# A planner's tables made to change along the stream: 40 places, 332 entries

## The chip, the cores and the metric

The kernel runs on one core of one Trainium2 chip. The metric is the device time of one execution in microseconds (us), as the median of several. The core has a matrix engine (TensorE, PE in the profile; PEld is its weight load), VectorE (DVE), ScalarE (ACT), GpSimd (POOL) and SyncE (SP), which only issues DMAs here. Matmuls write to PSUM, which has eight banks of 512 fp32 columns; everything else lies in SBUF.

## What is computed

Two layers; each is an attention block and then a mixer block, both with a residual, on x of 2048 rows and 448 columns (16 heads of 28):

```
x = x + A(layernorm(x), wqkv, wo)          # qkv, softmax(q k^T / sqrt(28)) v, wo
x = x + B(layernorm(x), w1, w2, w3, w4)    # twice, with the same weights
...
B(x): h  = gelu(layernorm(x) @ w1)
      hs = (the 4 column quarters of h, shifted by -1, +1, -2, +2 rows) @ w2
      x1 = x + hs
      x1 + gelu(layernorm(x1) @ w3) @ w4
```

The gelu is the one with tanh. Each layer has 16 x 2048 x 2048 exponentials in its softmax.

## The kernel before, in words

**Work and tiles.** The 2048 rows are 16 tiles of 128. A layer's queries are cut into five chunks of 4, 4, 4, 2 and 2 tiles (CHUNKS), its keys into chunks of two to four tiles (KC), its heads into four groups of four (g). ORDER lists the segments: for a chunk and a range of key tiles, one segment for each head group. A block is one key step of one head, 512 score columns wide; the segments laid end to end give the stream of 2048 blocks.

**Score units.** `t_scores` (L1631) walks through the stream and takes two or three blocks at a time as a unit: units of even number have three PSUM banks, those of odd number two. The scores are matmuls of 32 rows each (`score_ops`, L1510), and `t_exp` (L1733) gives a unit to ACT as one exp of 1536 or 1024 columns (L1748). Unit u waits for the exp of unit u - 2. `t_pv` (L1770) multiplies the exps by the values (L1765) in the order of the stream; the exp of unit u waits for the product of unit u - 6.

**Exps on VectorE.** Some blocks are taken out of the stream ahead of time (`ahead_of`, L1642) and get their exp as a polynomial on VectorE: one eviction (`d_first`, L1590, instruction L1592) and a chain of four more (L1619, L1621, L1623, L1626). Such a block either takes the third bank of an even unit (rates in R_RATE) or an extra bank (rates in D_RATE).

**The rest of the work** goes on between the units. `t_q` (L1386) loads four normed tiles transposed by a DMA (`load_xT`, L1230, instruction L1233) and starts `q_proj` (L1290) for each head group: projection on PE (L915 with wq_pad), eviction (L1307), square on GpSimd (L1248), a statistic on PE, and an add on VectorE (L1336), after which the block's scores can run. Keys go the same way with a maximum at the end (kmaxc, L1275); from the maxima `t_bias4` (L1430) makes a bias, and where a segment continues a chunk with further keys, `t_qp` (L1527) updates the query block by it (L1532). The mixer tiles are transposed one by one (`tr_dma`, L1123, instruction L1125). `t_mixB` (L2109) multiplies by w3, collects the results of up to four tiles in a buffer, h2T or a second one that lies in free slots of vaug and kT (h2W), and applies one gelu to it (L2202), for which ACT loads another table and then the exp table again. Some gelus are made from a tanh on ACT and VectorE steps instead (TANHW; L2019 to L2022), which needs no table.

**What sets the order.** Nothing is written in program order by hand. Every step is a Python generator that yields operations with a guessed duration. `Sched.run` (L466) keeps a planned time for each engine and at each step places the operation that can start first, by its priority where several can. RANK gives priorities by step and chunk, read when a step is started; R_RATE, D_RATE, RLO, RHI, DLO, DHI, DTH, DDTH and DWIN decide which blocks go to VectorE; PE_NORM chooses a way to normalise; Sched.DOUBT and DOUBT2 add a margin when an engine waits for another or for a DMA (`ready_at`, L452); Sched.EARLY lets a buffer be taken ahead of its data. `keep_pe_busy` (L405) puts filler matmuls (L2248, on the identity matrix) into planned gaps of PE, as TARGET and WIN ask. The result is one fixed list of instructions for each engine, with semaphores; the durations are then whatever the chip takes. Tables and knobs are constants for the whole plan. MOVES and WEAVE, which could edit the finished queues, are empty.

Of the kernel before, what the change touches and what calls it, by code (L numbers as in the profile page):

```python
# [264 lines left out]
class Sched:  # L265
    LAT = {"pe": 0.23, "act": 0.175, "dve": 0.145, "pool": 0.2, "sp": 0.2}
    OWN = {"pe": 0.0, "act": 0.15, "dve": 0.125, "pool": 0.05, "sp": 0.05}
    DOUBT = {"dma": 0.6, "pool": 0.4, "dve": 0.15, "act": 0.1}
    DOUBT2 = {"dma": 0.0, "pool": 0.0, "dve": 0.0, "act": 0.0, "pe": 0.0}
    EARLY = 0.25  # L270
    AGED = 1.0
    WIN = 2.3
    TARGET = 0.6
    LWIN = 2.8
    LOW = 0.0
    LCRED = 0.3
# [343 lines left out]
DPRIO = 3.393  # L620
DST = [('dve', 0.6), ('dve', 0.6), ('dve', 0.34), ('dve', 0.6)]
DSEG = 1
R_RATE = {2: 0.098, 3: 0.111, 5: 0.018, 6: 0.032, 13: 0.059, 20: 0.074, 22: 0.151, 25: 0.029, 29: 0.117, 31: 0.032, 32: 0.075, 35: 0.032, 37: 0.17, 38: 0.078, 39: 0.176, 41: 0.012, 42: 0.198, 43: 0.169, 44: 0.03, 45: 0.075, 46: 0.091, 54: 0.061, 56: 0.176, 59: 0.044, 62: 0.186, 33: 0.131, 63: 0.12, 16: 0.143, 23: 0.089, 18: 0.193, 27: 0.155, 61: 0.058, 49: 0.137, 30: 0.2, 53: 0.018, 0: 0.165, 40: 0.083, 8: 0.165, 1: 0.086, 26: 0.092, 48: 0.062, 60: 0.16, 55: 0.021, 52: 0.098, 4: 0.093, 9: 0.052, 15: 0.099, 10: 0.063, 28: 0.082, 7: 0.162, 47: 0.2, 12: 0.141}
RLO = 5
RHI = 7
RPRIO = 1
DWIN = 1.714
DTH = 0.403
XSHUT = (10, 76)
DLO = 6  # L630
DHI = 12
DPK = 2
DDTH = 1.502
UPRIO = 1.991
# [13 lines left out]
DURG = 1  # L648
FASTKV = 3
SMALL = [11, 12]  # L650
W_POS = (12, 6, 16, 6, 5, 10, 33, 26)
# [17 lines left out]
FMD = 0.83  # L669
FMO = 1.59  # L670
SWT = 0.103
Sched.DOUBT = {'dma': 0.8, 'pool': 0.6, 'dve': 0.05, 'act': 0.05}
Sched.LCRED = 0.3


# [4 lines left out]
def build_kernel(nc, A_x, A_wqkv, A_wo, B_x, B_w1, B_w2, B_w3, B_w4, out, n_layers=2):  # L680
# [85 lines left out]
    with st:  # L766
# [864 lines left out]
        def t_scores():  # L1631
            yield from seg_ready(0, segs[0][4])
            for b in BANKS[0:3]:
                yield ("acq", [b])
            yield ("reserve", "act", True)
            yield ("sig", ("start",))
            cur = -1
            pos = 0
            u = 0
            taken = {}  # L1640

            def ahead_of(si0, kb0, rates, lo, hi, used):  # L1642
                for ahead in range(lo, hi):
                    si, kb = si0, kb0 + ahead
                    while si < len(segs) and kb >= len(seg_kb[si]):
                        kb -= len(seg_kb[si])
                        si += 1
                    if si > si0 + DSEG or si >= len(segs):
                        return None
                    L, ch, g = segs[si][0:3]  # L1650
                    rate = rates.get(seg_b0[si] // 32, 0)
                    if not rate:
                        return None
                    js = [j for j in range(4) if (si, kb, j) not in home and j not in used]
                    if taken.get((si, kb), 0) >= DPK or not js:
                        continue
                    if taken.get((si, id(rates), 0), 0) >= rate * (kb + 1) * 4:
                        continue
                    if any(("k", L, g, kc_of(L, kt)) not in SC.events for kt in seg_kb[si][kb]):
                        return None  # L1660
                    if si > si0 and (("q", L, CHUNKS[L][ch][0] // 4, g) not in SC.events or (not segs[si][5] and ("qp", si) not in SC.events)):
                        return None
                    return (si, kb, js[0])
                return None

            def take(blk, rates, slot):
                home[blk] = pbuf(slot)
                taken[(blk[0], id(rates), 0)] = taken.get((blk[0], id(rates), 0), 0) + 1
                taken[blk[0:2]] = taken.get(blk[0:2], 0) + 1

            ringed = set()
            while True:
                if u == 1:
                    yield ("acq", ["b3"])
                    yield ("acq", ["b4"])
                if u >= 2:
                    yield ("wait", ("ex", u - 2))
                if u - 2 in ringed:
                    yield ("wait", ("dx", u - 2))
                un = []  # L1680
                rb = None
                lim = 3 - u % 2
                while pos < len(stream) and len(un) < lim:
                    if len(un) == 2 and rb is None and SC.load("dve", DWIN) < DTH:
                        rb = ahead_of(un[-1][0], un[-1][1], R_RATE, RLO, RHI, [b_[2] for b_ in un])
                        got = None
                        if rb is not None:
                            got = yield ("try", [xtra("y") + YS, xtra("pd") + PDS])
                        if got is not None:
                            take(rb, R_RATE, got[1])  # L1690
                            ringed.add(u)
                            break
                        rb = 0
                    blk = stream[pos]
                    pos += 1
                    if blk in home:
                        continue
                    home[blk] = ("pt", 5 * ((u // 2) % 3) + 3 * (u % 2) + len(un))
                    un.append(blk)
                    si = blk[0]  # L1700
                    if si != cur:
                        cur = si
                        yield ("sig", ("segstart", si))
                    yield from seg_ready(si, seg_kb[si][blk[1]])
                if not un:
                    break
                units.append(un)
                blks, banks = list(un), [b_ for b_ in unit_banks(u)]
                extra = []
                si0, kb0, _ = un[-1]  # L1710
                at[0], at[1] = si0, kb0
                if u in ringed:
                    blks.append(rb)
                    banks.append(2)
                    extra.append((rb, ("b2", got[0], got[1], u)))
                if SC.idle_share(8.0) >= FTH and SC.load("dve", DWIN) < DDTH:
                    blk = ahead_of(si0, kb0, D_RATE, DLO, DHI, [b_[2] for b_ in blks])
                    if blk is not None:
                        got = yield ("try", [MISC[0:2], xtra("y") + YS, xtra("pd") + PDS])
                        if got is not None:  # L1720
                            take(blk, D_RATE, got[2])
                            blks.append(blk)
                            banks.append(bi(got[0]))
                            extra.append((blk, got))
                yield from score_ops(blks, banks)
                for blk, got in extra:
                    yield ("spawn", d_first(blk, *got), 1 if len(got) == 3 else RPRIO)
                yield ("sig", ("st", u))
                u += 1
            units.append([])  # L1730
            yield ("sig", ("st", u))
# [377 lines left out]
        def t_mixB(L, ch, tiles, direct, pr):  # L2109
# [12 lines left out]
            if direct:  # L2122
                yield from tr_pe(slots, xt)
                for xs in slots:
                    yield ("rel", xs)
            wide = False
            hname = None
            small = L == 0 and tiles == SMALL
            if small:
                yield ("wait", ("kvfree",))  # L2130
                hb = vaug[:, 9:16, :].rearrange("p a b -> p (a b)").rearrange("p (f w) -> p f w", w=NW)
                hkey = [[("vaug", 9 + k) for k in range(f * NW // 512, (f * NW + NW - 1) // 512 + 1)] for f in range(14)]
            elif direct:
                hb, hkey = PT, [[("pt", f)] for f in range(14)]
            else:
                hname = yield ("acq", ["h2T", "h2W"] if ("xdone", 1) in SC.events else ["h2T"], [("xT", xt)])
                wide = hname == "h2W"
                if wide:
                    hkey = [[("vaug", 9 + f)] if f < 7 else [("kT", g, 2 + f) for g in range(4)] for f in range(14)]
                else:  # L2140
                    hb, hkey = h2T, [[("h2T", f), ("xst",)] for f in range(14)]
# [4 lines left out]
                return vaug[:, 9 + f, 128 * i:128 * i + 128] if f < 7 else kT[:, i, 128 * (2 + f):128 * (3 + f)]  # L2146

            late = []
            soft = TANHW.get((L, tiles[0]), 0) and not direct
            fps = 512 // NW  # L2150
            parts = [list(range(f, min(f + fps, 14))) for f in range(0, 14, fps)]
            if wide:
# [89 lines left out]
        def t_final():  # L2242
            for t in range(NT):
                yield ("wait", ("x2", 1, t))
            yield op("sp", 0.05, lambda e: e.nop(), deps=odmas)
# [44 lines left out]
        SC.spawn(t_extra(0, 16), 3)  # L2290
        SC.spawn(t_extra(1, 9), 3)
        SC.spawn(t_final(), 9)
        est = SC.run()

        def again(fn, k):
            return lambda e: [x for _ in range(k) for x in fn(e)]
# [63 lines left out]
```

## Time and profile before

| | |
|---|---|
| median of 3 runs | 1028.55 us (1028.09 to 1029.22) |
| profiled execution | 1028.86 us |
| its span, first to last instruction | 1027.1 us |
| mean granted TensorE clock | 1.000 |
| PE, DVE, ACT, POOL busy | 973.3, 823.3, 980.3, 293.1 us |
| instructions | 38497 |

The profile is that of one execution. A row of its groups reads: line, engine, operation, what is written from what, shapes and count; then busy us in sum and mean ns of one; then idle time of the engine just before these instructions, and who released it. A row of the timeline reads: start, duration, instruction, count, and in brackets the idle time before it with its releaser. A row of the stretches reads: from and to, length, busy us of PE, PEld, DVE, ACT and POOL with counts, the granted clock, the DMA share and GB/s. Matmuls overlap, so PE's busy time is more than its work.

The order in which a build puts the instructions of each engine can be read from the build without a run. It is used below for both kernels.

### The profile page before, as it was taken

Reading aid. Unit: us, or ns where it says so; the run is one execution under the profiler, and the core shown is the slowest. Engines: PE = TensorE matmul, PEld = TensorE weight load, DVE = VectorE, ACT = ScalarE, POOL = GpSimd, SP = SyncE. Lnnn points to the kernel's source line nnn. Section 1 sums busy time; section 2 is a strip of 40 time slices with the busy share of each in tenths; the row PEclk is TensorE's granted clock in tenths of the full one; section 3 lists DMA queues with packets and bytes.
Section 4 is the critical chain, followed back from the end, with each engine's and each line's share of the span. In section 5 each row is a group of like instructions: output and inputs, shape, how many; then the busy total and the mean of one; then the engine's idle time right before and its main releaser. Section 6 shows DMA issues by size and latency. Waiting matters only on the chain.

```text
span 1027.1 us, 38497 instructions
## 1 busy us (share of the span) xinstructions
PE 973.3 (95%) x17443; PEld 414.8 (40%) x17445; DVE 823.3 (80%) x1587; ACT 980.3 (95%) x898; POOL 293.1 (29%) x462
## 2 busy tenths in 40 slices
PE   8999999999998999999989999999999999999998
PEld 4332443443333344433343343344433343444465
DVE  7778989998887878778978688788888978887742
ACT  7999999999999999999997999999999999999942
POOL 2322121521435006144335122211535140423120
PEclk9999999999999999999999999999999999999999
DMA  4443341212311002321124017433302020121000
GB/s 120 130 115 105 98 107 50 56 36 53 89 42 33 14 23 61 72 44 37 38 72 77 25 44 174 121 85 92 75 13 38 23 60 27 34 64 37 13 21 25
DMA packets 99404, 62.73 MB, mean 61 GB/s; under 512 B 68712, under 2 KB 88552, under 8 KB 99240
## 3 DMA queue, kind: packets, MB, share of 16 engines
q1 hardware_dynamic: 99240, 60.27, 23.5%
q8 instruction: 136, 2.23, 1.0%
q14 instruction: 28, 0.23, 0.1%
HBM read 28.16 MB, written 16.76 MB: 44 GB/s over the span
## 4 chain that ended last, share of the span: by engine, by line
ACT 83%; PE 13%; DVE 2%; DMA 2%; issue 0%; DVEq 0%; SPq 0%; ACTq 0%
ACT PT L1748 77%; PE ps L915 9%; ACT h2T L2202 2%; PE ps L1510 2%; ACT fb L2021 2%; PE ps L1765 1%; PE ps L2248 1%; ACT L1748 1%; ACT L2202 1%; DMA xT<-xnd 1%; DMA xT<-xn 0%; DMA xnd<-xn 0%; PE ps L1139 0%; ACT vaug L2202 0%; ACT sq L1245 0%
## 5 line engine op out<-in xcount | busy, mean ns | idle before, releaser
L1748 ACT ACTIVATE PT<-ps 128x1024 bf16<-128x1024 f32 (+1 forms) x781 | 885.9, 1406 | 7.4 <-PE ps L1510 7.1
L1510 PE MATMUL ps<-qT,kT 32*128 32x512 bf16 (+1 forms) x2304 | 269.0, 335 | 29.4 <-ACT PT L1748 24.1
L1765 PE MATMUL ps<-PT,vaug 128*32 128x512 bf16 (+1 forms) x2423 | 202.7, 343 | 0.0
L2248 PE MATMUL ps<-ident 128*32 128x256 bf16 x4684 | 173.0, 276 | 1.8 <-POOL ident L1000 1.5
L1510 PEld LDWEIGHTS ps<-qT,kT 32*128 32x128 bf16 x2304 | 69.5, 91 | 257.2 <-ACT PT L1748 249.4
L915 PE MATMUL ps<-xT,w 128*32 128x512 bf16 (+3 forms) x2592 | 158.1, 341 | 3.2 <-DMA xT<-xn 1.5
L2248 PEld LDWEIGHTS ps<-ident 128*32 128x32 bf16 x4684 | 119.3, 98 | 38.8 <-issue 14.7
L1862 POOL TENSOR_TENSOR otn<-ub,fb 128x512 bf16<-128x512 f32 (+1 forms) x32 | 36.9, 1152 | 198.5 <-DMA fb<-rscr 198.4
L1765 PEld LDWEIGHTS ps<-PT,vaug 128*32 128x32 bf16 x2423 | 58.9, 94 | 76.8 <-issue 68.6
L1592 DVE TENSOR_SCALAR yd<-ps 128x512 int32<-128x512 f32 x106 | 72.6, 686 | 17.2 <-PE ps L1510 16.2
L915 PEld LDWEIGHTS ps<-xT,w 128*32 128x32 bf16 (+1 forms) x2592 | 61.6, 95 | 55.3 <-issue 23.9
L1619 DVE SCALAR_TENSOR_TENSOR fb<-yd 128x512 f32<-128x512 uint16 x106 | 78.5, 743 | 0.4
L1621 DVE SCALAR_TENSOR_TENSOR fb<-fb,yd 128x512 f32<-128x512 f32 x106 | 77.1, 728 | 1.0
L1626 DVE SCALAR_TENSOR_TENSOR PD<-yd,PD 128x512 int16<-128x512 int16 x106 | 74.8, 707 | 1.5
L915 PE MATMUL ps<-w,h2T 128*32 128x448 bf16 x1120 | 67.8, 354 | 1.0 <-ACT h2T L2202 0.6
L2180 DVE CAST h2T<-ps 128x512 bf16<-128x512 f32 (+1 forms) x70 | 44.5, 636 | 19.0 <-PE ps L915 18.3
L1248 POOL TENSOR_TENSOR sq<-kT 128x512 bf16<-128x512 bf16 (+2 forms) x32 | 31.1, 976 | 78.7 <-DVE kT L1262 61.3
L1248 POOL TENSOR_TENSOR sq<-qT 128x512 bf16<-128x512 bf16 x24 | 27.0, 1128 | 79.2 <-DVE qT L1307 73.9
L1623 DVE TENSOR_SCALAR PD<-fb 128x512 bf16<-128x512 f32 x107 | 46.8, 438 | 1.7
L1510 PE MATMUL ps<-wk_pad,kT 32*128 32x512 bf16 x256 | 37.8, 384 | 4.9 <-ACT PT L1748 4.0
L2019 POOL TENSOR_TENSOR fb<-hT 112x512 f32<-112x512 bf16 (+1 forms) x21 | 23.8, 1133 | 63.3 <-DVE hT L1991 25.6
L1765 PE MATMUL ps<-PD,vaug 128*32 128x512 bf16 (+1 forms) x136 | 40.7, 339 | 0.0
(195 smaller groups left out, 1215.1 us busy)
## 6 DMA issues: line engine op xcount, KB each, us to landing
uscr<-ub SPq DMA_DIRECT2D x28, 256.0 KB
ub<-uscr SPq DMA_DIRECT2D x28, 256.0 KB
fb<-rscr SPq DMA_DIRECT2D x24, 256.0 KB
xnd<-xn SPq DMA_DIRECT2D x28, 128.0 KB, 3.0
xd<-x_res SPq DMA_DIRECT2D x16, 224.0 KB, 3.4
x_res<-xd SPq DMA_DIRECT2D x16, 224.0 KB, 3.5
w<-in_B_w_dram SPq DMA_DIRECT2D x5, 448.0 KB, 8.8
obf<-in_A_x_dram SPq DMA_DIRECT2D x16, 112.0 KB, 2.8
```

Source lines behind the costliest of these rows:

```text
L915: r.append(e.matmul(out=out[c:c + w, :], lhsT=lhsT[:, c:c + w], rhs=rhs, start=start, stop=stop, tile_position=(0, c)))
L1248: return both("sq", 0.15 + NW * 0.0018, 0.07 + NW * 0.00104, lambda e: e.tensor_tensor(out=sq[:, si, 0:NW], in0=src, in1=src, op=ALU.mult) ...
L1510: yield op("pe", (0.005 + NW * 0.00042) / nc_, lambda e, i=i, kc=kc, j=j, g=g, qt=qt, a=a, NW=NW, bank=bank: e.matmul(out=ps[:, bank, i * ...
L1592: yield op("dve", c_ps(512), lambda e: e.tensor_scalar(out=y, in0=ps[:, bi(bank), :], scalar1=SCALE * L2E * FS, scalar2=-126.0 * FS, op0=A ...
L1619: yield op(D_[0][0], D_[0][1], lambda e: e.scalar_tensor_tensor(out=q, in0=lo, scalar=E2 / E3 * FS, in1=lo, op0=ALU.add, op1=ALU.mult), re ...
L1621: yield op(D_[1][0], D_[1][1], lambda e: e.scalar_tensor_tensor(out=q, in0=q, scalar=E1 / E3 * FS * FS, in1=lo, op0=ALU.add, op1=ALU.mult) ...
L1623: yield op(D_[2][0], D_[2][1], lambda e: e.tensor_scalar(out=pdt, in0=q, scalar1=E3 / FS ** 3, scalar2=E0, op0=ALU.mult, op1=ALU.add), rea ...
L1626: yield op(D_[3][0], D_[3][1], lambda e: e.scalar_tensor_tensor(out=pdt.bitcast(I16), in0=hi, scalar=128.0, in1=pdt.bitcast(I16), op0=ALU. ...
L1748: yield op("act", EXPC + n * w * 0.000833, lambda e, bk=bk, s0=s0, n=n, w=w: e.activation(out=PT[:, s0:s0 + n, 0:w], in_=ps[:, bk[0]:bk[0] ...
L1765: r.append(e.matmul(out=ps[32 * j:32 * j + 32, 5, 0:NW], lhsT=vaug[:, vs, 32 * (4 * g + j):32 * (4 * g + j) + 32], rhs=buf[:, s, i * NW:(i ...
L2180: ev = op("dve", c_ps(m * NW), lambda e, hr=hr, pv=pv: e.tensor_copy(out=hr, in_=pv), reads=[("ps", bi(b))], writes=hk, touch=[b])
L2248: return [e.matmul(out=ps[32 * c:32 * c + 32, bi(b), 0:256].rearrange("p (a n) -> p a n", n=128), lhsT=ident[:, 32 * c:32 * c + 32], rhs=i ...
```

## The change

A table TWEAK holds, for 40 score units from 6 to 774, a list of knobs and their new values, 332 in all: 170 in RANK, 162 in others (R_RATE, D_RATE, TANHW, PE_NORM, the windows and thresholds, Sched's margins and filler targets). `t_scores` applies the list when it comes to that unit, so that what is planned from there on is planned with the new values. `knobs` saves all of them before the plan and restores them behind it. One line moves: `soft` (a tile group made by tanh) is now settled before the buffer is taken, and such a group no longer takes the second buffer. No instruction's form is changed. In the changed file the lines from L673 on stand 34 lower and those behind the first line of the loop in t_scores 35 lower.

```diff
+KNOBS = ("RANK", "R_RATE", "D_RATE", "Q_LEAD", "PE_NORM", "TANHW", "W_POS", "DPRIO", "UPRIO", "DWIN", "DTH", "DDTH", "RLO", "RHI", "DLO", "DHI", "DURG", "FMD", "FMO")
+TWEAK = {
+  6: [('RANK', ('w', 1, 0), 1.401), ('D_RATE', 6, 0.105), ('RANK', ('m', 0, 3), 2.499), ('D_RATE', 1, 0.276), ('R_RATE', 0, 0.168), ('R_RATE', 1, 0.057), ('RANK', ('n', 0, 0), 0.821)],
...
+  230: [('R_RATE', 22, 0.22), ('Sched.DOUBT', 'dma', 0.46), ('R_RATE', 18, 0.09), ('RANK', ('a', 0, 3), 1.476), ('RANK', ('v', 0, 1), 2.946), ('RANK', ('b', 1, 3), 3.2), ('RANK', ('q', 1, 1), 2.248),
...
+  390: [('RANK', ('b', 1, 0), 1.132), ('Sched.DOUBT', 'dma', 0.33)],
...
+  486: [('Sched.WIN', None, 2.124), ('RANK', ('k', 1, 4), 1.253), ('RANK', ('e', 1, 0), 0.609), ('Sched.DOUBT', 'pool', 1.06), ('RANK', ('b', 1, 2), 3.186)],
...
+  774: [('FMD', None, 0.852)]}
+
+def tweak(items):
+    for (name, key, val) in items:
+        if name.startswith("Sched."):
+            if key is None:
+                setattr(Sched, name[6:], val)
+            else:
+                getattr(Sched, name[6:])[key] = val
+        elif key is None:
+            globals()[name] = val
+        else:
+            globals()[name][key] = val
+
+def knobs():
+    keep = {k: globals()[k] for k in KNOBS}
...
+    return back
@@ t_scores
             while True:
+                tweak(TWEAK.get(u, ()))
@@ t_mixB
+            soft = TANHW.get((L, tiles[0]), 0) and not direct
...
-                hname = yield ("acq", ["h2T", "h2W"] if ("xdone", 1) in SC.events else ["h2T"], [("xT", xt)])
+                hname = yield ("acq", ["h2T", "h2W"] if ("xdone", 1) in SC.events and not soft else ["h2T"], [("xT", xt)])
...
-            soft = TANHW.get((L, tiles[0]), 0) and not direct
@@ build_kernel
+        back = knobs()
         est = SC.run()
+        back()
```

More of the change, by code (lines that the diff above doesn't have):

```diff
@@ new lines, in tweak, with back @@
+def tweak(items):
[11 more added lines that the diff above has]
+    keep = {k: globals()[k] for k in KNOBS}
+    for k, v in keep.items():
+        if isinstance(v, dict):
+            globals()[k] = dict(v)
+    sch = {k: getattr(Sched, k) for k in ("TARGET", "WIN", "LWIN", "EARLY", "LCRED", "LOW", "AGED", "DOUBT", "DOUBT2")}
+    for k, v in sch.items():
+        if isinstance(v, dict):
+            setattr(Sched, k, dict(v))
+    def back():
+        globals().update(keep)
+        for k, v in sch.items():
+            setattr(Sched, k, v)
+    return back
```

1 line of the change is left out of this document (added).

## The prediction

> **What bounds the kernel now.** I read the page's busy times first, then the stretches, then ScalarE's waits, then the stall itself.
>
> ```profile
> PE 973.3 (95%) x17443; PEld 414.8 (40%) x17445; DVE 823.3 (80%) x1587; ACT 980.3 (95%) x898; POOL 293.1 (29%) x462
> ```
>
> PE and ACT are both at 95%, but PE's share holds filler (L2248), matmuls on the identity that only keep it active:
>
> ```profile
> L2248 PE MATMUL ps<-ident 128*32 128x256 bf16 x4684 | 173.0, 276 | 1.8 <-POOL ident L1000 1.5
> ```
>
> Without these 173.0 us PE is at 800 of 1027, so over the stream of score units ACT binds, and PE only where it is late. The stretches (columns: length, then busy us of PE, PEld, DVE, ACT, POOL) say where:
>
> ```profile
> 17.20:200.00 182.80, 173.72 (x2918) 68.85 (x2915) 155.21 (x322) 182.48 (x168) 44.70 (x58) 1.00 0.35 93
> ...
> 513.00:547.40 34.40, 31.23 (x649) 15.90 (x645) 24.77 (x48) 28.23 (x24) 13.72 (x18) 1.00 0.25 71
> ...
> 966.60:1027.10 60.50, 57.25 (x1298) 35.09 (x1298) 24.66 (x50) 26.77 (x38) 9.93 (x24) 1.00 0.09 24
> ```
>
> From 17 to 200 us ACT is busy 182.48 of 182.80; from 513 to 547 it loses 6.2; from 966.6 on PE is the bound (57.25 of 60.5) and ACT mostly waits. So the time is: head, ACT's sum of work in the stream plus its idle time there, and PE's sum of work in the tail. ACT's idle time between 17 and 967 us, by releaser and one by one:
>
> ```profile
> ACT PT L1748 <- PE ps L1510: 7.1, 4, 5.8
> ```
>
> ```profile
> 28.79 0.60 ACT L1245 ACTIVATE sq<-ps 128x512 bf16<-128x512 f32 x1 [0.27 <-PE ps L915]
> ...
> 422.54 1.02 ACT L1748 ACTIVATE PT<-ps 128x1024 bf16<-128x1024 f32 x1 [0.76 <-PE ps L1510]
> 423.80 4.63 ACT L1748 ACTIVATE PT<-ps 128x1536 bf16<-128x1536 f32 x4 [0.23 <-PE ps L1510]
> ...
> 529.36 1.45 ACT L1748 ACTIVATE PT<-ps 128x1536 bf16<-128x1536 f32 x1 [0.30 <-PE ps L1510]
> ...
> 547.41 1.45 ACT L1748 ACTIVATE PT<-ps 128x1536 bf16<-128x1536 f32 x1 [5.83 <-PE ps L1510]
> ```
>
> The whole stream has 7.39 us to win, and 5.83 of it is one stall. The other four make 1.56. Which unit stalls follows from the count of exps before it:
>
> ```profile
> L1748 ACT ACTIVATE PT<-ps 128x1536 bf16<-128x1536 f32 (+1 forms) x432 | 490.8, 1407 | 1.4 <-PE ps L1510 1.3
> ```
>
> 432 exps start before 547.3 us, so the late one is unit 432 (counted from 0): the first of layer 1, chunk 1, head group 0, which needs query block (1,1). Its chain in the timeline:
>
> ```profile
> 534.26 2.22 SPq L1233 DMA_TRANSPOSE xT<-xnd  x1
> ...
> 540.50 1.04 PE L915 MATMUL ps<-xT,wq_pad 128*32 128x512 bf16 x16
> ...
> 542.02 0.75 DVE L1307 TENSOR_SCALAR qT<-ps,bc 128x512 bf16<-128x512 f32 x1
> ...
> 542.85 1.04 POOL L1248 TENSOR_TENSOR sq<-qT 128x512 bf16<-128x512 bf16 x1 [1.29 <-DVE qT L1307]
> 543.07 1.95 PE L915 MATMUL ps<-xT,wq_pad 128*32 128x512 bf16 x32
> ...
> 545.57 0.40 PE L915 MATMUL ps<-sq,astatq 128*32 128x512 bf16 x4 [0.56 <-DVE qT L1307]
> ...
> 546.02 0.69 DVE L1336 TENSOR_TENSOR qT<-qT,ps 128x512 bf16<-128x512 bf16 x1
> ...
> 546.98 0.39 PE L1510 MATMUL ps<-qT,kT 32*128 32x512 bf16 x4
> ```
>
> The transposed load is issued at 534.26, the projection starts some 6 us later, and eviction, square, statistic and add follow one another until 546.7; the score starts at 546.98. The load came too late.
>
> **The change part by part.** The tables do not touch an instruction; they change the order and the choice of engine that the planner writes down. I compare the two built orders, and call *lag* the number of exps placed between an instruction and the one that needs it (one exp is 1407 ns on average in the row above).
>
> 1. *The stall at unit 432.* Before, query block (1,1) is loaded after exp 427 and its group-0 add (L1336) stands after exp 432 for scores of unit 432: lag 0. After, the load stands after exp 406, the four adds after exps 421, 424, 424 and 426, and their first user is unit 433: lag 12, about 17 us, against a chain of 12.7 us (534.26 to 546.98) of which the load's 21 exps more alone cover 29. It goes whole: **-5.83**. Behind it no query or key of a score has a lag of 0 or 1 until unit 526.
>
> 2. *Fewer exps on VectorE.* The polynomial exp (L1592 and the chain behind it) is built 100 times and not 108; 95 extra-bank ones stay, those that take a third bank from an ACT unit fall from 13 to 5. Both orders have 781 ACT exps, now 386 of 1536 and 395 of 1024 instead of 378 and 403. The rows by form:
>
> ```profile
> L1748 ACT ACTIVATE PT<-ps 128x1536 bf16<-128x1536 f32 x378 | 614.1, 1625 | 6.5 <-PE ps L1510 6.4
> L1748 ACT ACTIVATE PT<-ps 128x1024 bf16<-128x1024 f32 x403 | 477.8, 1201 | 0.8 <-PE ps L1510 0.8
> L2202 ACT ACTIVATE h2T<-h2T 128x7168 bf16<-128x7168 bf16 x3 | 18.5, 6181 | 0.0
> ...
> L2202 ACT ACTIVATE vaug<-vaug 128x3584 bf16<-128x3584 bf16 x1 | 3.2, 3183 | 0.0
> ```
>
> 8 x (1625 - 1201) = **+3.39** on ACT, the bound, with nothing to hide it. VectorE gets some 26 us back (eight chains of five instructions, each near 0.7 us) and gains no time, being at 80%.
>
> 3. *Other ACT work.* Table loads (14), tanh and small activations have equal counts. One 7168-wide gelu becomes two of 3584 in the stream, because another group got the second buffer: 2 x 3183 - 6181 = **+0.19**.
>
> 4. *The tail.* After the last scores stand 1190 PE instructions instead of 1206; the missing 16 are w3 matmuls of 512 columns, done earlier where PE has filler. Their price and those of the next check:
>
> ```profile
> 971.41 1.48 PE L915 MATMUL ps<-xT,w 128*32 128x512 bf16 x24
> ...
> 996.49 3.89 PE L915 MATMUL ps<-xT,w 128*32 128x256 bf16 x136
> ...
> 1015.73 8.12 PE L915 MATMUL ps<-w,PT 128*32 128x448 bf16 x168
> ```
>
> 16 x 1.48/24 = **-0.99**. A wait is added: the first w4 matmuls of the tail now read a 5632-wide gelu. PE gets to them after 52 of 512 columns, some 140 of 256, 32 of 448 and small ones: 3.2 + 4.0 + 1.5 + 1.5, near 10 us past the last score. ACT gets there after 1.8 us of last exp, a table load, three evictions and the gelu (6181 x 5632/7168 = 4.86):
>
> ```profile
> L2176 ACT ACTIVATE h2T<-ps 128x512 bf16<-128x512 f32 x7 | 4.2, 596 | 10.7 <-PE ps L915 10.7
> ...
> L2202 ACT ACT_TABLE_LOAD x6 | 7.7, 1283 | 0.1
> ```
>
> 1.8 + 1.28 + 1.79 + 4.86 = 9.7. It fits by 0.3; I take 0, and 1 us as its upper end. Everything on PE is queued behind it if it doesn't.
>
> 5. *A new tight place.* The query update (L1532) for unit 526 (layer 1, chunk 0, keys from 11) stands after exp 526: lag 0, the only one left beside the start. It needs the last kmaxc, placed after exp 524, and five small VectorE steps:
>
> ```profile
> L1532 DVE TENSOR_SCALAR qT<-qT,db 128x512 bf16<-128x512 bf16 x28 | 8.7, 349 | 0.2
> ...
> L1275 DVE TENSOR_REDUCE kmaxc<-ps 128x1 f32<-128x384 f32 x8 | 4.4, 554 | 1.3 <-PE ps L915 1.0
> ```
>
> 0.55 + 0.35 + five steps, which I estimate at under 0.35 each from the wider L1532: under 2.7 us, for a room of two to three exps (2.8 to 4.2). So it just fits. Ends: 0, and 5.83 by the row of the other lag-0 place. I take **+0.5**, between the small stalls of 0.23 and 0.76.
>
> 6. *Transposes.* PE's loads by transpose with lag 3 or less go from 14 to 18, but the one with lag 0 (after exp 420) goes; margins for DMA fall in the tables from 0.8 to 0.46 and 0.33. Before, PE waited for such loads only thus:
>
> ```profile
> PE ps L915 <- DMA xT<-xn: 1.5, 1, 1.5
> PE ps L915 <- DMA xT<-xnd: 1.3, 1, 1.3
> ```
>
> and ACT lost 0.76 + 0.23 and 0.30 by it. Ends: -1.3 and +3. I take 0: the 1.56 us of small stalls stay.
>
> 7. *Filler.* 4164 instead of 4684 matmuls: nothing waits for them, 0. In every stretch the granted clock is 1.00. [...]
>
> Sum: -5.83 + 3.39 + 0.19 - 0.99 + 0.5 = -2.74. The profiled execution took 1028.86 (span 1027.1), so 1026.1; the median is 0.31 lower, so **1025.8**.
>
> **Rivals.**
> - *Late transposes* (item 6): three more PE waits of 1.3 to 1.5, each with about 1.0 of ACT idle as at 422 us: +3.0, 1028.8, no change. For it: more short lags, lower margins. Against: before met 14 short lags with two such waits. Idle that returns in small pieces elsewhere reads the same.
> - *The stall moves* (item 5): unit 526 waits as 432 did, 5.83 instead of 0.5: 1025.8 + 5.33 = 1031.1, slower. It decides when the update ends about 5 us after ACT runs dry; for that the K projection or kmaxc must slip by four exps. Against: the chain is short and its K tiles stand after exps 514 to 519.
> [...]
> - *Nothing gained*, if the adds at 421 were not what unit 433 waits for. The order excludes it.
>
> **How the numbers follow.** A measurement tells about 0.2%, 2 us: faster is below 1026.5, slower above 1030.6. Forecast 0.46 (1023.8 to 1026.5), late transposes or scattered idle 0.32, moved stall 0.16, clock 0.06 (half of it slower). So faster 0.46, same 0.35, slower 0.19. Low end: items 5 and the 1.56 at zero, 1025.8 - 2.1 = 1023.7; high end: the moved stall, 1031.1.
>
> **What would show it.** ACT: 386 and 395 exps at 1625 and 1201 ns; no idle over 1 us near unit 433; idle in the stream near 2 us; at unit 526 an idle of 0.5 released by PE behind L1532. Tail from last exp to end 53 us and not 54. PE waits for DMA in sum below 4 us, clock 1.00 throughout. It is wrong if ACT's idle in the stream is above 4 us, wherever, or if exps are longer.

## The result, and the profile after

The changed kernel took 1025.95 us in the median (10 runs, 1024.58 to 1028.92), the kernel before 1028.75 beside it (10 runs, 1027.77 to 1030.77): ratio 0.9972, 95% interval 0.9962 to 0.9982. The forecast was 1025.8 with -2.74 for the change; the medians differ by -2.80. The profiled execution after took 1024.58 with a span of 1022.9. In the changed file L1748 is L1783, L1510 is L1544, L915 is L949, L1532 is L1566, L2248 is L2283.

Busy times of the page, then filler and exps by form, of the kernel after:

```profile
PE 960.4 (94%) x16925; PEld 399.8 (39%) x16925; DVE 798.5 (78%) x1557; ACT 983.0 (96%) x898; POOL 284.3 (28%) x453
...
L2283 PE MATMUL ps<-ident 128*32 128x256 bf16 x4164 | 156.3, 276 | 1.5 <-POOL ident L1034 1.5
```

```profile
L1783 ACT ACTIVATE PT<-ps 128x1536 bf16<-128x1536 f32 x386 | 625.3, 1620 | 1.8 <-PE ps L1544 1.8
L1783 ACT ACTIVATE PT<-ps 128x1024 bf16<-128x1024 f32 x395 | 470.5, 1197 | 0.5 <-PE ps L1544 0.4
```

ACT is busier than before (983.0 against 980.3), with more wide exps as built, and yet the kernel is shorter. Where the time went shows when the span is cut at the start of the first exp and the end of the last. Stretches of before and of after (length, then busy us of PE, PEld, DVE, ACT and POOL):

```profile
17.06:972.88 955.82, 908.28 (x16039) 374.25 (x16036) 791.13 (x1496) 947.91 (x850) 280.61 (x425) 1.00 0.25 61
972.88:1027.10 54.22, 50.97 (x1190) 32.45 (x1178) 20.74 (x42) 20.50 (x32) 7.20 (x19) 1.00 0.08 24
```

```profile
15.89:969.85 953.96, 897.67 (x15536) 360.37 (x15536) 769.15 (x1469) 951.04 (x851) 269.14 (x414) 1.00 0.25 61
969.85:1022.90 53.05, 50.10 (x1174) 32.53 (x1162) 18.10 (x38) 20.19 (x31) 9.80 (x21) 1.00 0.07 22
```

In the stream ACT works 951.04 - 947.91 = 3.13 us more, and is idle 953.96 - 951.04 = 2.92 instead of 955.82 - 947.91 = 7.91: 4.99 less. The tail is 1.17 shorter. The head is 1.17 shorter too, but the orders there are equal, and in the twelve profiles of this study the first exp starts anywhere from 15.7 to 17.7 us: the profiled execution had a short one. Without it the spans differ by -3.0.

All waits of ACT from 16 to 970 us after, one by one (start, length, then in brackets the idle time):

```profile
27.62 0.60 ACT L1279 ACTIVATE sq<-ps 128x512 bf16<-128x512 f32 x1 [0.27 <-PE ps L949]
404.99 10.49 ACT L1783 ACTIVATE PT<-ps 128x1536 bf16<-128x1536 f32 x9 [1.21 <-PE ps L1544]
427.27 4.62 ACT L1783 ACTIVATE PT<-ps 128x1536 bf16<-128x1536 f32 x4 [0.33 <-PE ps L1544]
887.42 1.02 ACT L1783 ACTIVATE PT<-ps 128x1024 bf16<-128x1024 f32 x1 [0.39 <-PE ps L1544]
888.70 4.62 ACT L1783 ACTIVATE PT<-ps 128x1536 bf16<-128x1536 f32 x4 [0.26 <-PE ps L1544]
```

The stall of 5.83 is gone and nothing took its place: neither at unit 433 nor at unit 526. There the chain from the last maximum of the keys to the small exp fct on ACT (L1489), which scales what a continued segment has summed so far, reads thus in the timeline:

```profile
653.94 0.56 DVE L1309 TENSOR_REDUCE kmaxc<-ps 128x1 f32<-128x384 f32 x1
654.53 0.17 DVE L1471 TENSOR_REDUCE k<-kmaxc 128x4 f32<-128x20 f32 x1
655.27 0.16 DVE L1503 TENSOR_TENSOR dbc<-bcb 128x4 f32<-128x4 bf16 x1
656.25 0.22 DVE L1505 TENSOR_SCALAR db<-dbc,cols 128x4 f32<-128x4 f32 x1
656.51 1.93 DVE L1566 TENSOR_SCALAR qT<-qT,db 128x512 bf16<-128x512 bf16 x7
657.25 0.52 ACT L1489 ACTIVATE fct<-dbc 128x4 f32<-128x4 f32 x1
```

dbc is ready at 655.43, ACT comes to fct at 657.25 and does not wait (no bracket). The room is 1.8 us: one or two exps.

### The profile page after: what moved, and what is told of

Read it like the earlier page. It is cut to its first block, busy times and chain, and to the rows that moved or that the text cites. A ratio compares the mean times of both kernels' runs of the same rounds, so it can differ in the third digit from the quotient of the medians.

```text
span 1022.9 us, 37404 instructions
## 1 busy us (share of the span) xinstructions
PE 960.4 (94%) x16925; PEld 399.8 (39%) x16925; DVE 798.5 (78%) x1557; ACT 983.0 (96%) x898; POOL 284.3 (28%) x453
## 4 chain that ended last, share of the span: by engine, by line
ACT 90%; PE 7%; DVE 1%; DMA 1%; issue 0%; SPq 0%; DVEq 0%; ACTq 0%
ACT PT L1783 83%; PE ps L949 6%; ACT h2T L2237 2%; ACT fb L2056 2%; ACT L1783 1%; ACT L2237 1%; DMA xT<-xnd 1%; PE ps L1544 1%; ACT vaug L2237 1%; ACT kT L2237 1%; DMA xnd<-xn 0%; DMA PT<-in_A_wqkv_dram 0%; PE ps L1800 0%; ACT sq L1279 0%; PE ps L940 0%
## 5 line engine op out<-in xcount | busy, mean ns | idle before, releaser
L1783 ACT ACTIVATE PT<-ps 128x1024 bf16<-128x1024 f32 (+1 forms) x781 | 890.8, 1406 | 2.3 <-PE ps L1544 2.2
L1544 PE MATMUL ps<-qT,kT 32*128 32x512 bf16 (+1 forms) x2304 | 268.9, 335 | 39.3 <-ACT PT L1783 30.5
L1800 PE MATMUL ps<-PT,vaug 128*32 128x512 bf16 (+1 forms) x2432 | 200.1, 340 | 0.0
L1544 PEld LDWEIGHTS ps<-qT,kT 32*128 32x128 bf16 x2304 | 69.5, 91 | 276.3 <-ACT PT L1783 269.0
L949 PE MATMUL ps<-xT,w 128*32 128x512 bf16 (+4 forms) x2656 | 169.5, 345 | 1.4 <-DVE PD L1657 1.2
L2283 PE MATMUL ps<-ident 128*32 128x256 bf16 x4164 | 156.3, 276 | 1.5 <-POOL ident L1034 1.5
L2283 PEld LDWEIGHTS ps<-ident 128*32 128x32 bf16 x4164 | 105.2, 97 | 40.9 <-issue 21.3
L1626 DVE TENSOR_SCALAR yd<-ps 128x512 int32<-128x512 f32 x97 | 66.5, 686 | 34.2 <-PE ps L1544 33.2
L949 PEld LDWEIGHTS ps<-xT,w 128*32 128x32 bf16 (+1 forms) x2656 | 63.0, 95 | 62.7 <-issue 32.0
L1800 PEld LDWEIGHTS ps<-PT,vaug 128*32 128x32 bf16 x2432 | 62.9, 95 | 48.0 <-issue 38.0
L1655 DVE SCALAR_TENSOR_TENSOR fb<-fb,yd 128x512 f32<-128x512 f32 x97 | 69.2, 714 | 0.8
L1660 DVE SCALAR_TENSOR_TENSOR PD<-yd,PD 128x512 int16<-128x512 int16 x97 | 67.9, 700 | 1.0
L1653 DVE SCALAR_TENSOR_TENSOR fb<-yd 128x512 f32<-128x512 uint16 x97 | 67.8, 703 | 0.5
L949 PE MATMUL ps<-w,h2T 128*32 128x448 bf16 x1008 | 64.4, 355 | 0.7 <-ACT h2T L2237 0.7
L1897 POOL TENSOR_TENSOR otn<-ub,fb 128x512 bf16<-128x512 f32 (+1 forms) x23 | 26.5, 1154 | 136.8 <-DMA fb<-rscr 129.4
L1140 POOL TENSOR_SCALAR vpe<-mv 128x1 f32<-128x1 f32 (+2 forms) x21 | 8.3, 393 | 149.3 <-DVE mv L1135 149.3
L1544 PE MATMUL ps<-wk_pad,kT 32*128 32x512 bf16 x256 | 39.0, 384 | 7.3 <-ACT PT L1783 6.2
L1657 DVE TENSOR_SCALAR PD<-fb 128x512 bf16<-128x512 f32 x98 | 41.5, 424 | 1.0
L949 PE MATMUL ps<-xT,wq_pad 128*32 128x512 bf16 x512 | 39.3, 382 | 0.7 <-DVE vaug L1386 0.7
```

What stands on the lines that cost most here:

```text
L949: r.append(e.matmul(out=out[c:c + w, :], lhsT=lhsT[:, c:c + w], rhs=rhs, start=start, stop=stop, tile_position=(0, c)))
L1544: yield op("pe", (0.005 + NW * 0.00042) / nc_, lambda e, i=i, kc=kc, j=j, g=g, qt=qt, a=a, NW=NW, bank=bank: e.matmul(out=ps[:, bank, i * ...
L1626: yield op("dve", c_ps(512), lambda e: e.tensor_scalar(out=y, in0=ps[:, bi(bank), :], scalar1=SCALE * L2E * FS, scalar2=-126.0 * FS, op0=A ...
L1653: yield op(D_[0][0], D_[0][1], lambda e: e.scalar_tensor_tensor(out=q, in0=lo, scalar=E2 / E3 * FS, in1=lo, op0=ALU.add, op1=ALU.mult), re ...
L1655: yield op(D_[1][0], D_[1][1], lambda e: e.scalar_tensor_tensor(out=q, in0=q, scalar=E1 / E3 * FS * FS, in1=lo, op0=ALU.add, op1=ALU.mult) ...
L1660: yield op(D_[3][0], D_[3][1], lambda e: e.scalar_tensor_tensor(out=pdt.bitcast(I16), in0=hi, scalar=128.0, in1=pdt.bitcast(I16), op0=ALU. ...
```

## The experiments

Theory (of the prediction): ACT binds in the stream, PE in the tail; the time is ACT's work, plus its idle time where something stands too close behind what it needs, plus PE's work in the tail. Rivals: the lags don't matter (idle moves elsewhere); ACT doesn't bind everywhere; filler decides through the clock. Each kernel is the changed one with one edit. Medians stand beside 9 to 23 runs of the kernel before on the same chip (1028.91 to 1029.04). The last two columns are us of the profiled execution, the stream from the start of the first exp to the end of the last, the tail from there on; that execution is not always a middling one (half filler 1027.10, first 20 places 1041.09).

| kernel | us (median) | ratio to before, 95% | ACT busy / idle in the stream | tail |
|---|---|---|---|---|
| before | 1028.75 | | 947.9 / 7.9 | 54.2 |
| after | 1025.95 | 0.9972 (0.9962 to 0.9982) | 951.0 / 2.9 | 53.1 |
| first 11 places | 1064.59 | 1.0344 (1.0326 to 1.0363) | 948.0 / 40.2 | 56.4 |
| late load | 1040.56 | 1.0113 (1.0095 to 1.0132) | 953.5 / 16.4 | 53.8 |
| no third bank | 1040.96 | 1.0112 (1.0097 to 1.0128) | 955.0 / 14.7 | 53.4 |
| no filler | 1054.35 | 1.0255 (1.0236 to 1.0274) | 955.6 / 25.4 | 53.1 |
| old planner margins | 1051.41 | 1.0215 (1.0199 to 1.0232) | 952.2 / 28.9 | 53.7 |
| fewer VectorE exps | 1029.32 | 1.0004 (0.9991 to 1.0018) | 954.0 / 4.1 | 52.8 |
| half filler | 1029.97 | 1.0011 (0.9996 to 1.0025) | 950.8 / 4.4 | 53.0 |
| first 20 places | 1044.97 | 1.0165 (1.0140 to 1.0190) | 949.7 / 19.0 | 53.6 |
| two DMA margins | 1040.99 | 1.0120 (1.0105 to 1.0136) | 952.5 / 16.1 | 54.0 |
| more places | 1026.62 | 0.9981 (0.9970 to 0.9991) | 951.8 / 4.6 | 51.7 |

ACT's work spans 8 us over all of them, its idle time 37: the idle time decides. Two prices can be read from ACT's timelines. Where exps are queued, one of 1536 columns takes 1.34 us from the end of the one before it to its own, and one of 1024 takes 0.92: 0.43 us for a bank of 512 columns, 0.06 for a unit. An exp that follows a wait takes 0.11 us more (1.45 for 1536 columns), so the waits make a part of the work too. In first 11 places, no third bank, fewer VectorE exps, first 20 places and two DMA margins one exp has 512 columns only; the expectations count it as 1024.

### The first 11 places alone

```diff
 TWEAK = {6: [...], 22: [...],
...
   166: [...],
-  230: [...], 246: [...],
...
-  774: [...]}
+  }
```

> The first 11 of the 40 places (units 6 to 166) stay, the other 29 are left out. By the order built: the stall's cause at unit 432 is gone (no query of a score there has lag 0), 371 exps of 1536 columns and 413 of 1024 on ACT (784 units), 110 exps on VectorE, and a tail with 52.7 us of PE work by widths instead of 50.4 before and 49.4 after. My sum against before: stall -5.83, exps -0.2, tail +2.3, one tight place +0.5, so about -3.2: ratio 0.9969 to before, about 1025.5 us, like after. Rival one, the gain of the change comes from tables late in the stream (less idle in small pieces): then this kernel is at or above before, 1028 to 1031 us. Rival two, the tail is hidden: then -5.5, 1023.3 us.

Measured: 1064.59. All three missed. The stall at unit 432 is gone as said, but ACT waits elsewhere, and most at fct:

```profile
657.01 0.62 DVE L2253 TENSOR_TENSOR x_res<-x_res,ps 128x448 f32<-128x448 f32 x1 [0.60 <-PE ps L949]
...
664.19 3.54 SPq L1267 DMA_TRANSPOSE xT<-xnd  x1
...
667.97 3.04 PE L949 MATMUL ps<-xT,wk_pad 128*32 128x384 bf16 x64 [2.57 <-issue]
...
673.73 1.18 DVE L1309 TENSOR_REDUCE kmaxc<-ps 128x1 f32<-128x384 f32 x2
...
676.94 0.21 ACT L1489 ACTIVATE fct<-dbc 128x4 f32<-128x4 f32 x1 [15.36 <-DVE dbc L1503]
```

This is the seam between the layers. The last residual add of layer 0 (L2253) is followed by a layer norm, a write to DRAM, a transposed load, the projection of the keys, the maxima and the bias; fct is the last of them. From add to fct it is 676.94 - 657.01 = 19.9 us, and ACT runs nothing in the 15.36 us before fct: the exps behind it in its list go on at 678.05. In the order built only 3 exps lie between add and fct here; before it was 21, after 20. My lags looked only at the queries and keys that a score reads, and not at fct. The other 24 us of idle time are 15 smaller waits, six of them, 16.5 in sum, for products (L1800). So the first quarter of the table isn't where the gain is.

### The load of query block (1,1) put back to late

```diff
-Q_LEAD = {..., (1, 1): 13, ...}
+Q_LEAD = {..., (1, 1): 0, ...}
```

> The changed kernel with one knob put back to a late value: query block (1,1) is loaded only when its segment starts (Q_LEAD of it 13 to 0), so that the add for unit 433 has lag 0 again, as before had for unit 432. By the order built also 387 and 396 exps on ACT (95 on VectorE instead of 100, +2.6 us at 0.43 us per bank of 512 columns and 0.06 per exp) and a tail of 49.8 instead of 49.4 (+0.4). My theory: ACT stands idle near unit 433 for 4 to 7 us, and the kernel takes 1025.95 + 5.8 + 3.0 = 1034.8 us (1033 to 1036). Rival, the stall is no net cost, since ACT's idle time is made good later: no more than the 3.0, 1029 us, or the idle is there and other idle goes.

Measured: 1040.56, 14.6 more than after. The timeline, and the count of exps up to that point, of this kernel:

```profile
556.45 25.88 ACT L1783 ACTIVATE PT<-ps 128x1024 bf16<-128x1024 f32 x23 [8.07 <-PE ps L1544]
```

```profile
L1783 ACT ACTIVATE PT<-ps 128x1536 bf16<-128x1536 f32 (+1 forms) x433 | 494.8, 1393 | 3.8 <-PE ps L1544 3.7
```

433 exps before it: the late one is unit 433, with 8.07 us, as the order said. The rival is out, but my range was too low as well: idle time rose by 13.5 in all, against the 5.8 expected. Some 2 of that lie ahead of 500 us, where the orders are still equal and the clock fell twice for 3.4 us (at 405.4 and 453.2; 0.997 in the mean of this execution). Two more waits, 2.29 and 1.64, come behind the stall, where the edit changed what was planned.

### No third bank for VectorE

```diff
-R_RATE = {2: 0.098, 3: 0.111, ...}
+R_RATE = {}
```
and no R_RATE entry in TWEAK.

> The changed kernel with R_RATE empty in the first table and along the stream: no exp takes a third bank for VectorE. By the order built 391 and 391 exps on ACT (386 and 395 in the changed kernel), VectorE 94 instead of 100, tail 49.8 instead of 49.4 us. My theory (ACT binds and each bank of 512 columns moved to it costs 0.42 us): 8 banks and one unit more, 1955 against 1947, so +3.4, and the tail +0.4: 1029.8 us (1028.8 to 1031). Rival, ACT does not bind everywhere (VectorE's chains late or PE late): no difference to the changed kernel or a gain, 1025 to 1027 us.

Measured: 1040.96, far above both. ACT's work rose by 3.9. That it is near the +3.4 is luck: with the exp of 512 columns ACT took over 6 banks and one unit and not 8 banks (VectorE's exps fell from 100 to 94), 2.6 us at 0.43 a bank, and most of the rest is that 23 exps follow a wait and not 12. Idle time rose by 11.7, and 7.26 us of it are again at fct, which here stands 8 exps behind the add:

```profile
671.12 0.20 ACT L1489 ACTIVATE fct<-dbc 128x4 f32<-128x4 f32 x1 [7.26 <-DVE dbc L1503]
```

So it doesn't price the exps; it gives a second point for fct: lag 3, 15.4 us; lag 8, 7.3; lag 20, none.

### No filler

```diff
     def keep_pe_busy(self, until):
-        if self.fill is None:
-            return
+        return
```

> The changed kernel without any filler matmul (4164 of 256 columns on the identity left out); all other instructions stand in the same order on every engine. My theory: nothing waits for filler, so 1025.95 us within 1 us, if the granted clock stays at 1.00; ACT's idle in the stream stays near 2.5 us. [...]

Measured: 1054.35, 28.4 us more and not within 1: the granted clock did not stay at 1.00, its mean in the profiled execution was 0.898. Three stretches of 3.4 us, one behind the other, of this kernel:

```profile
212.06:215.47 3.41, 3.05 (x35) 0.83 (x35) 3.40 (x7) 3.41 (x4) 1.04 (x1) 1.00 0.01 2
215.47:218.89 3.42, 1.15 (x13) 0.33 (x13) 3.42 (x7) 3.42 (x5) 0.00 (x0) 1.00 0.02 2
218.89:222.30 3.41, 2.40 (x16) 0.50 (x16) 3.34 (x7) 3.41 (x5) 0.00 (x0) 0.50 0.41 108
```

PE runs 13 matmuls in the second, 1.15 us busy, and in the third the granted clock (third column from the right) is 0.50. The trace has 63 such half windows between 25 and 1000 us, 215 us in all. The median rose by 28.4 us, 0.45 for each window of 3.4, or 0.13 per us: PE has slack in the stream (857.75 us busy of 981.03), and only part of the delay reaches ACT, as many small waits. Of the 28.9 us between the spans, 22.5 are idle time of ACT, 4.6 its work (49 exps follow a wait and not 12) and 1.8 the head:

```profile
L1782 ACT ACTIVATE PT<-ps 128x1024 bf16<-128x1024 f32 (+1 forms) x781 | 894.9, 1351 | 24.9 <-PE ps L1543 24.4
```

### The planner's margins and targets as before

```diff
 TWEAK = {
...
-  390: [('RANK', ('b', 1, 0), 1.132), ('Sched.DOUBT', 'dma', 0.33)],
+  390: [('RANK', ('b', 1, 0), 1.132)],
...
```
and so for each entry whose name begins with Sched.

> The changed kernel without its entries for the planner's margins and filler targets (those whose name begins with Sched); ranks, rates and windows stay. By the order built: 385 and 396 exps on ACT (one bank of 512 columns less), tail 48.9 us instead of 49.4, no lag-0 place but unit 526, but the small exp on ACT that needs the last maximum of the keys (fct, L1489) stands only 9 exps behind the residual add of layer 0's last tile, on which its chain begins; in the changed kernel 20, in the runs of the first 11 places and of no third bank 3 and 8, where ACT waited 15.4 and 7.3 us for it. From these two rows: the chain takes about 18 us, an exp 1.2. Theory A, that wait and the terms of my sum: 18 - 9 x 1.2 = 7.2 at fct, -0.4 -0.5 for exps and tail: 1032 us (1030 to 1035). Theory B, the planner's own end is right but for a constant: it ends 22.8 us later than that of the changed kernel (with a wait of 8.5 at fct and one of 12.6 at a table load after exp 238, which my lags do not look at), so 1048.7 us (1047 to 1051).

Measured: 1051.41. Theory A is right at fct (lag 9, 7.05 us, expected 7.2) and wrong in the sum, 19 us too low. What my lags miss most are the two waits behind exp 238, 3.36 and 8.70: 12.1 us, where the planner had 12.6. What ACT meets there is a tanh activation (L2056) and then an exp, not the table load that I named. B is 2.7 short.

```profile
300.73 0.63 ACT L2056 ACTIVATE fb<-fb 112x512 f32<-112x512 f32 x1 [3.36 <-DVE fb L2055]
...
310.06 2.37 ACT L1783 ACTIVATE PT<-ps 128x1536 bf16<-128x1536 f32 x2 [8.70 <-PE ps L1800]
...
678.50 0.21 ACT L1489 ACTIVATE fct<-dbc 128x4 f32<-128x4 f32 x1 [7.05 <-DVE dbc L1503]
```

### Fewer exps on VectorE, in the last segments only

```diff
-D_RATE = {..., 59: 0.182, 61: 0.113, 63: 0.154, ...}
+D_RATE = {...}
```

> The changed kernel with the rates of VectorE exps set to nothing in the last segments only (D_RATE 59, 61 and 63), so that all orders up to some 880 us stay as they are. 388 and 396 exps on ACT instead of 386 and 395 (8 banks of 512 columns and 3 units more), VectorE 93 instead of 100, tail 48.9 instead of 49.4 us. My theory (ACT binds there too; a bank costs 0.42 us, a unit 0.06): +3.5 - 0.5 = +3.0, 1029.0 us (1028 to 1030). Rival, ACT is not the bound in the last segments, or VectorE's chains cost it something: 1025 to 1027 us. By the planner's own end it would be +2.6.

Measured: 1029.32, +3.4 against the expected +3.0. The orders are equal up to 880 us, but the sum behind the +3.0 is not what made the +3.4:

```profile
16.98:975.13 958.15, 902.15 (x15560) 362.42 (x15556) 751.19 (x1438) 954.02 (x854) 263.16 (x411) 1.00 0.24 61
975.13:1027.90 52.77, 49.80 (x1162) 32.75 (x1154) 19.38 (x39) 19.79 (x30) 8.69 (x20) 1.00 0.07 22
```

ACT's work is 954.02 - 951.04 = 2.98 more. With the exp of 512 columns it took over 7 banks and 3 units and not 8 banks; at 0.43 and 0.06 they make 3.2. Idle time adds 1.2, and the tail loses 0.3. But 2.0 us of the idle time lie between 968 and 973 us, where the clock is at 0.5 (966.0 to 972.9; 0.996 in the mean of this execution). The two of the twelve executions with a clock of 1.000 took 1025.80 and 1026.52, against a median of 1025.69 for the three of after at 1.000; the other ten ran at 0.995 to 0.998 and took 1028.39 to 1032.67. So the work went to ACT, but most of the +3.4 goes with the clock, and the rival isn't out: whether ACT binds in the last segments stays open.

### Half the filler

```diff
-            return [e.matmul(out=ps[32 * c:32 * c + 32, bi(b), 0:256].rearrange("p (a n) -> p a n", n=128), ...
-                             rhs=ident[:, :].unsqueeze(1).to_broadcast([128, 2, 128]), ...
+            return [e.matmul(out=ps[32 * c:32 * c + 32, bi(b), 0:128], ...
+                             rhs=ident[:, :], ...
```

> The changed kernel with every filler matmul 128 columns wide instead of 256, in the same places: all queues are the same, PE's filler work is half. Without any filler the clock stood at 0.5 in 63 windows of 3.4 us and the kernel took 28.4 us more, 0.45 us for each. There, windows at half clock follow on windows in which the matmuls' columns, counted from the trace at full clock, fill less than about 0.38 of the time. With half of the filler 4 to 8 windows of the changed kernel fall below 0.38 to 0.40, with all of it one or two. Theory A, the clock goes by such windows: 3 to 6 more half windows, a clock near 0.99, +1.5 to +3 us: 1027.5 to 1029 us. Theory B, of my prediction: nothing waits for filler and half of it holds the clock: 1025.95 within 0.6 us. Theory C, each filler counts alike: half of 28.4 us, 1040 us.

Measured: 1029.97, 4.0 more: more than A's 3, and neither B nor C. The twelve executions ran at clocks from 0.983 to 0.998, and the time goes roughly with it: 1033.66 and 1034.31 at 0.983 and 0.987, 1027.10 at 0.998. The median clocks, 0.9925 here and 0.998 after, stand for some 11 us more at half clock (an estimate), so each us of it cost about 0.35 here. So filler isn't free to remove, though far from alike: C, which counts each one the same, is out.

### The first 20 places alone

```diff
 TWEAK = {6: [...],
...
   358: [...],
-  390: [...], 406: [...],
...
-  774: [...]}
+  }
```

> The changed kernel with the first 20 of the 40 places alone (units 6 to 358); the others, from 390 on, left out. By the order built: 380 and 402 exps on ACT (4 banks less, one unit more than the changed kernel: -1.6), tail 50.1 instead of 49.4 us (+0.65), fct 19 exps behind the residual add (no wait), lag 0 at unit 526 and lag 1 at unit 531. Theory A, the terms of my sum: 1025.95 - 1.0 + 0.5 = 1025.5 us, so the second half of the table brings nothing (1024.5 to 1027). Theory B, the planner's own end: 7.1 us later than the changed kernel's, with ACT waiting 3.2 us before unit 526 and 5.6 before unit 592: 1033 us (1032 to 1035), so the second half of the table takes away waits.

Measured: 1044.97, above both. First the clock in 40 slices from the page of this kernel, then the two waits that B named, from the timeline; the second is longer:

```profile
PEclk9999999999999999999999999999689999999999
```

```profile
659.73 74.26 ACT L1783 ACTIVATE PT<-ps 128x1536 bf16<-128x1536 f32 x66 [2.76 <-PE ps L1800]
...
743.24 2.36 ACT L1783 ACTIVATE PT<-ps 128x1536 bf16<-128x1536 f32 x2 [9.25 <-PE ps L1800]
```

The clock is at 0.5 from 733.5 to 760.8 us (0.987 in the mean of this execution). ACT's longer wait, 9.25 us, begins at 734.0, just behind the fall; five smaller waits, 4.7 us in sum, follow until 761. The planner, which knows no clock, had 5.6 us at this place, so the order makes a part of the wait; how much of the rest goes with the half clock is not separated here. The five executions go with the clock: 1041.09 at 0.987, 1050.22 at 0.974, or about 0.34 us for each us at half clock. So the later half of the table keeps waits away.

### Two DMA margins put back

```diff
-  230: [..., ('Sched.DOUBT', 'dma', 0.46), ...],
+  230: [...],
...
-  390: [('RANK', ('b', 1, 0), 1.132), ('Sched.DOUBT', 'dma', 0.33)],
+  390: [('RANK', ('b', 1, 0), 1.132)],
```

> The changed kernel without two of its 332 entries: the planner's margin for a PE operation that waits for a DMA stays at 0.8 us (0.46 from unit 230 and 0.33 from unit 390 are left out). By the order built the load of query block (1,1) is late again (lag 0 at unit 432, as before the change), the last residual add of layer 0 stands 8 exps ahead of fct instead of 20, ACT has 388 and 394 exps (4 banks and one unit more, +1.5 us), the tail 50.1 instead of 49.4 us. Theory A, idle follows the lags that the runs have shown: 7.3 us at fct (lag 8: 7.26 in the run with no third bank), 5.8 to 8.1 at unit 432, +1.5, +0.7: 1041 to 1044 us. Theory B, of my prediction: these margins move only the transposed loads by a little, -1.3 to +3: 1025 to 1029 us.

Measured: 1040.99, A's lower end; B is out. The waits are where the lags put them, after 432 exps and at fct, but the sum is partly luck: unit 432 waits 2.90 and not 5.8 or more, and 2.65 us behind fct were not expected:

```profile
545.31 18.18 ACT L1783 ACTIVATE PT<-ps 128x1536 bf16<-128x1536 f32 x16 [2.90 <-PE ps L1544]
...
667.70 0.21 ACT L1489 ACTIVATE fct<-dbc 128x4 f32<-128x4 f32 x1 [7.42 <-DVE dbc L1503]
670.55 87.33 ACT L1783 ACTIVATE PT<-ps 128x1536 bf16<-128x1536 f32 x77 [2.65 <-PE ps L1544]
```

The head is equal to after's here and the clock 1.00 throughout, so the spans close: +13.2 idle, +1.4 work on ACT, +0.9 tail make the 15.5 between 1038.4 and 1022.9. Without these two entries the other 330 give a kernel 1.2% slower than before. The first 20 places alone hold the first of the two (0.46) and not the second, and there ACT waits neither at unit 432 nor at fct: the first is enough to keep both waits away.

### More places for an earlier mixer

```diff
 TWEAK = {
...
+  541: [('RANK', ('m', 1, 1), 1.334)], 552: [('D_RATE', 45, 0.009)],
...
+  779: [('RANK', ('e', 1, 3), 0.6)]}
```

> The changed kernel with 19 entries more at 16 places from unit 541 on, chosen so that more of the last mixer tiles is done before the last scores: queues are as in the changed kernel up to there; 386 and 395 exps and 100 on VectorE as there, tail by widths 48.05 instead of 49.41 us (52 fewer groups of four matmuls of one kind, other widths more). Theory A, PE is the bound in the tail: -1.4, 1024.6 us (1023.5 to 1025.7), with ACT's idle in the stream as in the changed kernel. Rival, the work done earlier makes PE or VectorE late in the stream, where ACT is the bound, or one more gelu group there costs two table loads of 1.28 us: 1026 to 1029 us.

Measured: 1026.62, in the rival's range and above A's: no gain over after (the intervals of the two ratios overlap). The tail fell by 1.37 to 51.68, as A said. The stream took it back: ACT's work rose by 0.7 and its idle time by 1.7, 1.3 of it between 769 and 774, where the clock is at 0.5 from 766.3 to 773.1. The stretches around it:

```profile
762.53:766.30 3.77, 2.39 (x22) 0.59 (x19) 3.09 (x7) 3.77 (x4) 3.50 (x6) 0.99 0.57 83
766.30:769.70 3.40, 2.82 (x25) 0.74 (x29) 2.90 (x7) 3.11 (x4) 2.18 (x8) 0.50 1.21 112
769.70:773.10 3.40, 3.40 (x42) 1.11 (x38) 2.18 (x5) 2.58 (x3) 3.40 (x9) 0.50 0.16 34
```

None of its eleven executions had a clock above 0.997. No version found beats the changed kernel.

## Why the prediction was right

1. *The stall at unit 432* (-5.83): right. Nothing waits there after; with the load late again, unit 433 waits 8.07, with the two margins put back unit 432 waits 2.90. The size goes with how late the chain is, so 5.83 holds for before alone.
2. and 3. *VectorE exps and gelu* (+3.58): 0.45 too high. ACT's work grew by 3.13. The exps are right: each counted from the end of the instruction before it, they grew by 3.36 (+3.39 forecast), and the difference of the two means, 424 ns, is what a bank costs. The gelus grew by 0.08 and not 0.19, and the tanh activations shrank by 0.30, which no run explains; after and half filler, with the same order on ACT, differ by 0.27.
4. *The tail* (-0.99): -1.17. The added wait for the 5632-wide gelu does not show.
5. *The tight place at unit 526* (+0.5): 0. But the reason given was thin: I looked at the update of the queries, and the instruction that ACT meets first is fct, on the same chain. fct had 1.8 us of room. The update, which I put at under 2.7 us from the start of the last kmaxc, ended after 2.9. The rival "the stall moves" has the right mechanism and place: four edited kernels lose 7.0 to 15.4 us there (lag 3: 15.4; lag 8: 7.3 and 7.4; lag 9: 7.0; lags 19 to 21: none).
6. *Transposes* (0): +0.84. Idle time outside the big stall was 7.91 - 5.83 = 2.08 before and is 2.92 after, mostly the 1.21 at 405 us, behind a transposed load that PE can use 5.9 us after its issue (397.68 to 403.56). The term lies within its ends, and the step was wrong in what it took the margins for: the order on which items 1 and 5 rest hangs on one of them.
7. *Filler* (0): right in the profiled execution, not quite in the median. 7 of the 10 executions after had a clock of 0.997 or 0.998, of before 19 of 47 were below 1.000; the three after at 1.000 have a median of 1025.69, 0.3 below that of all ten; the 28 of before at 1.000 have 1028.8, 0.2 below that of all 47. So the clock cost after about 0.1 us more than before, an estimate from these medians. The chance of 0.06 that the clock falls had no row of before behind it: all show 1.00. Where the clock fell in the later runs, each us at half clock cost 0.13 us (no filler) to about 0.35 (half filler, first 20 places).

The forecast change and that of the medians differ by 0.06 us, and that is luck: the misses, -0.45 -0.18 -0.5 +0.84 +0.1, nearly cancel. What was right is the size of the three large terms (stall, exps, tail) and that the order, not the tables, was read. What was not earned is the trust in the order: the lags that I counted would not have seen the 15.4 us at fct, had they been there.

Beside the terms stood a number that I had not used: the planner's own end, from its guessed durations. It is 1015.8 us for before and 1012.9 for after, -2.9. Median less planned end is 13.0 and 13.1 for these, 12.7, 12.9 and 11.9 for late load, no third bank and two DMA margins, 13.8 for fewer VectorE exps, and more where the clock fell: 15.3 for more places, 15.8 for old margins, 20.6 for the first 11, 25.0 for the first 20. Half filler and no filler have after's planned end, and are 17.1 and 41.5 above it. So the planned end has most of the waits, but not the clock.

## What to carry to other kernels

Where one engine binds and its queue is in order, price a reordering by two sums, the work of that engine and its waits, and look for the waits at every instruction in that queue, the small ones too, not only at the operands of the big ones. Count how much of the binding engine's work lies between the start of a chain and its end (after, 20 exps, some 23 us, for a chain of 21), and put the lags of several kernels beside their waits: here 15.4 us at lag 3, 7.0 to 7.4 at 8 and 9, none from 19 on. When work on a second engine is cut, filler included, look at its granted clock as well: without filler PE's fell here from 1.000 to 0.898, and the kernel took 28.4 us more.

## What the runs showed of the hardware

The granted clock of PE stands at 1.0 or 0.5 in these traces. Stretches at 0.5 that stand above lasted 3.4 us (no filler, 218.89 to 222.30), 6.8 (more places, 766.3 to 773.1) and 27.3 (first 20 places, 733.5 to 760.8). A matmul takes longer there, by the modelled ends: in more places a group of four matmuls (w and hT, 448 columns) takes 0.37 us at 1.0 (from 758.39) and 0.57 at 0.5 (from 767.42). The busy time of PE alone does not tell the places with a fall from one without. PE was busy for 1.15 of 3.42 us ahead of the fall in no filler, and for 2.39 of 3.77 ahead of that in more places; but in after it was busy for only 1.88 of 3.41 (401.20 to 404.61), and the clock stayed at 1.00 there and behind it:

```profile
401.20:404.61 3.41, 1.88 (x47) 0.85 (x39) 1.69 (x5) 2.57 (x3) 3.18 (x9) 1.00 1.14 121
404.61:408.02 3.41, 3.41 (x65) 1.26 (x68) 2.94 (x5) 3.04 (x3) 3.33 (x6) 1.00 0.35 74
```

The share of about 0.38 in the expectation for half the filler is my estimate from the trace of no filler; with it a clock near 0.99 was expected, and the median was 0.9925. The clock of one and the same kernel differs from execution to execution: 1.000 in three of after's ten, 0.997 or 0.998 in the other seven. What makes it fall is not settled by these runs.
